# A planned attention and two-layer kernel: the first two batches regrouped by head halves and tile pairs, and the weight loads reordered

## The chip, the cores and the metric

The kernel runs on one core of a Trainium2 chip. The metric is the device time of one execution in microseconds (us). The engines named below are TensorE (PE: matmuls and transposes; PEld is its weight load), VectorE (DVE), ScalarE (ACT), GpSimd (POOL) and SyncE (SP), which only starts transfers. Transfers are started by SP (inputs of the attention, transposes by DMA) and by POOL (weights, which are cast from float32 to float16 on the way, and stores).

## The reference

```python
def phi(x, c, s):
    r = np.maximum(x, 0.0)
    return np.concatenate([r * c, r * s], axis=-1)
q_p = phi(q, cos_w, sin_w)
k_p = phi(k, cos_w, sin_w)
kv = np.einsum('bhsf,bhsd->bhfd', k_p, v)
z = np.sum(k_p, axis=2)
num = np.einsum('bhsf,bhfd->bhsd', q_p, kv)
den = np.einsum('bhsf,bhf->bhs', q_p, z)[..., None] + 1e-06
x = num / den          # 8 batches, 8 heads, 576 tokens, 64 per head
h = x @ w_in           # 4608 tokens x 512, 512 x 2048
g = h * np.cos(h)
out = g @ w_out        # 2048 x 512
```

The attention is linear: per head, one 128 x 65 product of k and v (the 65th column sums k), and a numerator with its denominator for every tile of tokens. Its result, transposed, is the input of a two-layer network.

## The kernel before

The kernel is written as a list of steps. Each step is added to a `Plan` with its engine, the functions that issue its instructions, and the keys that it reads and writes. Two tables in the source, `STARTS` (one whole number per step) and `ENGS` (one letter per step, for steps that either of two or three engines can do), give the order: steps are issued in the order of `STARTS`, on the engine of `ENGS`. Every engine runs its own instructions in that order and waits, in order, for what each needs.

Tokens: a batch has 576 tokens, four full tiles of 128 and a fifth of 64. Raw q, k and v lie in `km`, `qm` and `vm` (float32, one buffer each, used by all batches in turn), so a batch's k can be loaded only when the batch before has prepared its own. Each raw tensor of a batch is loaded by two transfers per group of heads, `go4` (line 339) and `go5` (line 336).

A batch's attention:
- `prep` (lines 368 on ACT, 369 on DVE) makes relu(x) times cos or sin, float16, into `KQ`; one instruction per tile and per cos or sin, over 8 heads or over a half of them.
- `cast_v` (382 ACT, 383 DVE, 384 POOL) casts v to float16.
- `kv` multiplies k and v over five tiles for 8 heads: 40 matmuls (line 397), and copies the result to `kvz`.
- `q_pe` transposes q of one tile on PE, 8 transposes (428), and copies it to `qT` (435 ACT, 437 DVE). Batches 2 and later do it by DMA (`q_dma`, 441).
- `num` makes the numerators of one tile (464), 8 matmuls in two banks; a normalisation on DVE follows, three instructions: the denominator (481), its reciprocal (483) and the product (485) into `XN`.
- `x_pe` transposes the result, 4 transposes (519), and a copy puts it into `xT` (522 to 524).

The network: `layer1` for batches 0 and 1 runs 16 groups of 8 matmuls (575), each group with a cosine on ACT (547) and a product on DVE (549). `layer2_plain` is the second layer of batch 0: for each of four tiles 16 matmuls (878) in two runs, over the first `WQ` quarters of `w_out` and over the rest; the first run is copied by ACT (886), the second added by DVE (889). Batches 1 to 8 use a form with seven products (`layer1_fast`, `layer2`), whose sums of weights are made on DVE: `w_out_sums` (901) and `w_in_sums` (660).

Before the weights come, PE runs dummy matmuls (`warm`, line 1041): 28 at the start, 17 after the first q transposes, and small groups between the numerators.

Loads of weights: `w_in` and `w_out` come in four quarters each, started by POOL. Small copies on POOL (1055, 1058, 1076, 1083) write one element of the destination first, so that a load waits for what the copy reads. `hold_raw` (1098) holds batch 1's inputs in the same way until `GATE1`, a quarter of a weight, has landed; `part_of_w_out` (1115) holds the last quarters of `w_out` until q or k of batch 1 has landed. Before, the order is: q, k, v of batch 0; four quarters of `w_in`; two of `w_out`; k, q, v of batch 1 (held until the quarter 2 of `w_in` is there); the other two of `w_out`.

The option `HH` chooses between `first_attention` (empty, as before) and `first_attention_halves`.

Of the kernel before, what the change touches and what calls it, by code (L numbers as in the profile page):

```python
# [13 lines left out]
F16 = mybir.dt.float16  # L14
# [3 lines left out]
OPT = dict(F16=0, WS2=[3, 1], HQ=[1, 0, 1], AQ=0, W2F=0, WQ=2, L2F=0, WFI=None, XPE=[0, 1, 2, 3, 4], FAST1={3:  # L18
           2, 4: 2, 5: 2, 6: 4, 7: 4, 8: 4}, MODE={}, HH='', LD=[['k', 0], ['v', 0], ['q', 0], ['k', 1], ['v',
           1], ['q', 1]], NB=[['A0', 'A1'], ['A0', 'A1', 'M0']], XB=[['B3'], ['B3', 'M1']], W0=5, W1=6,  # L20
           WF=[[2, 2, 2, 2], [2, 2, 0, 0]], HOLD=['k', 1], P0=0, RAW1=2, WO2=1, H1=0, DA=0, W2=0, SQ=0, NUZ=1)
# [169 lines left out]
def kernel(  # L191
# [84 lines left out]
    TR = ppool.tile([P, SM], F32, name="TR")  # L276
# [339 lines left out]
    FAST1 = OPT["FAST1"]  # L616
# [845 lines left out]
```

## Time and profile before

| | us |
|---|---|
| median of 3 runs | 281.5 (281.26 to 281.94) |
| the profiled execution | 281.42 |
| its span | 279.6 |
| PE busy | 272.5 |
| DVE busy | 236.4 |
| ACT busy | 210.0 |
| POOL busy | 83.4 |

The granted clock of PE is 1.00 over the whole span. The page gives busy times as shares of the span; in its rows of 40 slices a digit is the busy share of a slice of about 7 us in tenths. In rows of the timeline the first number is the start in us from the start of the span, the second the time taken, then the engine, the source line, the operation, what it writes and reads, how many instructions are merged, and in brackets the idle time before it and what ended it. An engine name with a q (SPq, POOLq) is the starting of a transfer. In rows of the DMA view the last number is the time in us from the starting of a transfer to its landing. In rows of windows, each engine has its busy time and its number of instructions, and the last three numbers are the granted clock, the busy share of the DMA engines and GB/s.

### The profile page before, as it was taken

The page shows a single profiled execution, that of the slowest core. Times are in us where ns is not written, and L with a number is a line of the kernel's source. Part 1 is how long each engine was busy: PE and PEld are TensorE (multiplying, and loading weights), DVE is VectorE, ACT ScalarE, POOL GpSimd, SP SyncE. Part 2 cuts the span into 40 slices and gives each one's busy share as a digit, 9 for nine tenths or more (in the row PEclk, how much of TensorE's full clock was granted, in tenths as well). Part 3 has the DMA queues.
Part 4 walks back from the last instruction along what each step waited for, and adds up shares of the span by engine and source line. Part 5 has one row for each costly group of instructions (what it writes and reads, how often), then busy time and mean ns, then how long its engine had stood idle before and what let it go on. Part 6 is the DMA issues. An engine that isn't in the chain of part 4 may idle for free.

```text
span 279.6 us, 6829 instructions
## 1 busy us (share of the span) xinstructions
PE 272.5 (97%) x2698; PEld 215.5 (77%) x2698; DVE 236.4 (85%) x442; ACT 210.0 (75%) x363; POOL 83.4 (30%) x104
## 2 busy tenths in 40 slices
PE   8999999999999999999999999999999999999993
PEld 2567867787966677769776878789988888888882
DVE  1767698989999999999999998989989879873952
ACT  2756699879998897788989978995758696776330
POOL 1340020030502101520440045132534372399210
PEclk9999999999999999999999999999999999999999
DMA  6999999989999999969999998739756495697125
GB/s 209 337 205 205 361 218 258 338 282 181 324 303 263 242 230 264 285 200 287 216 249 265 212 260 283 109 104 142 161 76 146 102 159 102 150 146 123 75 77 150
DMA packets 80223, 58.03 MB, mean 208 GB/s; under 512 B 43200, under 2 KB 77248, under 8 KB 80192
## 3 DMA queue, kind: packets, MB, share of 16 engines
q1 hardware_dynamic: 68960, 39.99, 59.3%
q0 software_dynamic: 10496, 17.04, 29.3%
q10 hardware_dynamic: 736, 0.57, 0.7%
q8 instruction: 21, 0.34, 0.5%
q14 instruction: 10, 0.08, 0.1%
HBM read 36.75 MB, written 11.80 MB: 174 GB/s over the span
## 4 chain that ended last, share of the span: by engine, by line
PE 92%; ACT 3%; DVE 2%; issue 1%; POOL 0%; ACTq 0%; POOLq 0%
PE M L953 34%; PE M L736 14%; PE M L608 11%; PE M L575 9%; PE TR L736 6%; PE ATT L1041 5%; PE ATT L464 3%; PE M L878 3%; PE ATT L397 3%; PE TR L608 2%; ACT KQ L368 1%; DVE XN L485 1%; PE M L428 1%; ACT V L382 0%; ACT ch L547 0%
## 5 line engine op out<-in xcount | busy, mean ns | idle before, releaser
L953 PEld LDWEIGHTS <-gT 128*128 128x128 f16 x560 | 53.9, 98 | 8.3
L953 PE MATMUL M<-w_out_sb,gT 128*128 128x256 f16 x448 | 57.1, 273 | 0.0
L549 DVE TENSOR_TENSOR gT<-M,ch 128x512 f16<-128x512 f32 x73 | 48.5, 684 | 5.9 <-ACT ch L547 5.7
L547 ACT ACTIVATE ch<-M 128x512 f32<-128x512 f32 x75 | 43.4, 596 | 12.2 <-PE M L575 5.4
L368 ACT ACTIVATE KQ<-km,CS 128x512 f16<-128x512 f32 x57 | 38.5, 718 | 1.6 <-DMA km<-in_k_dram 1.6
L964 ACT ACTIVATE ost<-M 128x512 f32<-128x512 f32 x41 | 24.3, 596 | 18.0 <-PE M L953 13.0
L368 ACT ACTIVATE KQ<-qm,CS 128x512 f16<-128x512 f32 x46 | 31.5, 721 | 4.0 <-DMA qm<-in_q_dram 4.0
L608 PE MATMUL M<-xT,w_in_sb 128*128 128x512 f16 x136 | 33.8, 379 | 0.0
L953 PE MATMUL M<-T,S 128*128 128x256 f16 x256 | 32.3, 273 | 0.0
L384 POOL CAST V<-vm 128x1024 f16<-128x1024 f32 (+1 forms) x18 | 15.8, 904 | 51.6 <-DVE den L481 21.6
L736 PEld LDWEIGHTS <-w_in_sb 128*128 128x128 f16 x288 | 27.3, 98 | 4.8 <-issue 0.3
L575 PE MATMUL M<-xT,w_in_sb 128*128 128x256 f16 x256 | 30.3, 273 | 0.3 <-DVE gT L549 0.3
L953 PEld LDWEIGHTS <-S 128*128 128x128 f16 x256 | 24.8, 98 | 4.1 <-DVE S L929 0.2
L575 PEld LDWEIGHTS <-w_in_sb 128*128 128x128 f16 x256 | 24.4, 98 | 3.9 <-issue 0.5
L748 DVE TENSOR_TENSOR Z<-M,Z 128x512 f32<-128x512 f32 x31 | 21.1, 687 | 4.3 <-PE M L736 3.2
L608 PEld LDWEIGHTS <-w_in_sb 128*128 128x128 f16 x160 | 14.9, 98 | 12.2
L549 POOL TENSOR_TENSOR gT<-Z,ch 128x512 f16<-128x512 f32 x5 | 6.3, 1268 | 56.6 <-ACT ch L547 20.0
L485 DVE TENSOR_TENSOR XN<-ATT,rec 128x512 f16<-128x512 f32 x32 | 22.1, 692 | 1.1
L464 PEld LDWEIGHTS <-qT 128*128 128x128 f16 (+1 forms) x320 | 14.8, 101 | 5.6 <-issue 3.5
L759 ACT ACTIVATE ch<-Z 128x1024 f32<-128x1024 f32 x12 | 12.7, 1057 | 6.9 <-DVE Z L748 4.9
L744 ACT ACTIVATE Z<-M 128x512 f32<-128x512 f32 x26 | 15.2, 596 | 3.4 <-PE M L736 2.4
L464 PE MATMUL ATT<-kvz,qT 128*128 128x65 f16 (+1 forms) x288 | 16.0, 195 | 0.8 <-DVE XN L485 0.5
(152 smaller groups left out, 519.3 us busy)
## 6 DMA issues: line engine op xcount, KB each, us to landing
out_dram<-ost POOLq DMA_DIRECT2D x38, 256.0 KB, 4.1
qm<-in_q_dram SPq DMA_DIRECT2D x8, 640.0 KB, 6.3
km<-in_k_dram SPq DMA_DIRECT2D x8, 640.0 KB, 7.1
qm<-in_q_dram SPq DMA_DIRECT2D x8, 512.0 KB, 5.7
km<-in_k_dram SPq DMA_DIRECT2D x8, 512.0 KB, 5.9
vm<-in_v_dram SPq DMA_DIRECT2D x6, 640.0 KB, 6.0
vm<-in_v_dram SPq DMA_DIRECT2D x6, 512.0 KB, 4.4
w_in_sb<-in_moe_w_in_dram POOLq DMA_DIRECT2D x4, 512.0 KB, 7.5
```

Source lines behind the costliest of these rows:

```text
L368: fn = {"ACT": lambda: nc.scalar.activation(out=out_, in_=in_, func=AF.Relu, scale=sc), "DVE": lambda: nc.vector.tensor_scalar(out=out_, i ...
L384: "POOL": lambda: nc.gpsimd.tensor_copy(out=out_, in_=in_)}
L464: nc.tensor.matmul(bank[hb][ps, hh * D1:(hh + 1) * D1], lhsT=x[:, h, :], rhs=z[:, h, :], start=True, stop=True)
L485: nc.vector.tensor_tensor(out=split(x16[n][:, hs, :], k), in0=A[:, :, :, 0:D], in1=split(rec[n][:, hs], k).unsqueeze(3).broadcast_to((P, k ...
L547: act(0.5, due, lambda: nc.scalar.activation(out=ch[c], in_=bank, func=AF.Sin, bias=math.pi / 2.0, scale=1.0), [key], [("ch", c)])
L549: mul(due, 0.61, lambda q: q.tensor_tensor(out=dst, in0=bank if len(dst.shape) == 2 else bank.rearrange("p (j s) -> p j s", j=dst.shape[1] ...
L575: nc.tensor.matmul(M1[m][:, jj * 2 * P:(jj + 1) * 2 * P], lhsT=w_in_sb[:, cc, j * P:(j + 1) * P], rhs=X[:, cc, ts], start=(cc == 0), stop= ...
L608: nc.tensor.matmul(M, lhsT=w_in_sb[:, cc, j * P:(j + 1) * P], rhs=X[:, cc, :], start=(cc == 0), stop=(cc == NCT - 1))
L736: nc.tensor.matmul(bank[0][:, j * TH:(j + 1) * TH], lhsT=a(cc, j), rhs=b[:, cc, :], start=(first and j == 0 and cc == 0), stop=(last and j ...
L748: dve(0.61, due + 0.3, lambda: nc.vector.tensor_tensor(out=dst, in0=bank[0], in1=dst, op=ALU.add), [bank[1], key], [key])
L953: nc.tensor.matmul(bank[0][:, tt * MH:(tt + 1) * MH], lhsT=a[:, j, tt * P:(tt + 1) * P], rhs=b[:, j, :], start=(first and (apart or tt == ...
L964: act(0.5, due, lambda: nc.scalar.activation(out=dst, in_=view(bank), func=AF.Copy), [bank[1]], dk)
```

## The change

The options and the two tables are new, and the order of the steps with them. The new options are `HH='kv'`, `P0=1`, `H1=2`, `WQ=3`, `W2F=2`, `RAW1=4`, `HOLD=['k', 0]`, another order `LD` of batch 0's loads and other numbers of dummy matmuls (`WF`). In words:

- Batch 0 runs `first_attention_halves`. q is prepared and transposed for all heads as before. k and v are prepared for heads 0 to 3 first; their product (`kv_half`, 20 matmuls) follows, then the numerators of a pair of tiles for these heads (`num_pair`), one normalisation for the pair, and four transposes and one copy for the pair (`x_pair`); then the same for heads 4 to 7. In the plan's order the two halves are interleaved. Both halves of the bank `ATT` hold a pair.
- Batch 1 uses `kv_half` and `num_pair` as well, and its steps may go to ACT or DVE.
- The first layer of batches 0 and 1 takes the groups of quarters 0 and 1 for the first half of the tokens, then for the second half, then quarters 2 and 3.
- Three quarters of `w_out` are loaded ahead of batch 1's inputs, which are held until the first quarter of `w_out` is there. The last quarter is held until the first transfer of batch 1's q has landed, through two copies on POOL.
- Batch 0's second layer is split into runs of 12 and 4 matmuls.
- The dummy matmuls are five groups of four and small groups of two.
- The code gains an option `FW`, which is not used.

Loads of batch 0 stay in the order q, k, v with v in two halves of heads.

```diff
-OPT = dict(F16=0, WS2=[3, 1], HQ=[1, 0, 1], AQ=0, W2F=0, WQ=2, L2F=0, WFI=None, XPE=[0, 1, 2, 3, 4], FAST1={3:
-           2, 4: 2, 5: 2, 6: 4, 7: 4, 8: 4}, MODE={}, HH='', LD=[['k', 0], ['v', 0], ['q', 0], ['k', 1], ['v',
-           1], ['q', 1]], NB=[['A0', 'A1'], ['A0', 'A1', 'M0']], XB=[['B3'], ['B3', 'M1']], W0=5, W1=6,
-           WF=[[2, 2, 2, 2], [2, 2, 0, 0]], HOLD=['k', 1], P0=0, RAW1=2, WO2=1, H1=0, DA=0, W2=0, SQ=0, NUZ=1)
+OPT = dict(F16=0, WS2=[3, 1], HQ=[1, 0, 1], AQ=0, FW=None, W2F=2, WQ=3, L2F=0, WFI=None, XPE=[0, 1, 2, 3, 4],
+           FAST1={3: 2, 4: 2, 5: 2, 6: 4, 7: 4, 8: 4}, MODE={}, HH='kv', LD=[['q', 3], ['k', 3], ['v', 0],
+           ['v', 1]], NB=[['A0', 'A1'], ['A0', 'A1', 'M0']], XB=[['B3'], ['B3', 'M1']], W0=5, W1=6, WF=[[2,
+           2], [2, 2]], HOLD=['k', 0], P0=1, RAW1=4, WO2=1, H1=2, DA=0, W2=0, SQ=0, NUZ=1)
 STARTS = (
...
 ENGS = (
...
-        warm(28, 9.05)
+        if OPT["FW"]:
+            for i, n in enumerate(OPT["FW"]):
+                warm(n, 7.5 if i == 0 else 0.2157 * n)
+        else:
+            warm(28, 9.05)
...
-        warm(17, 3.67, rd=[("TR", 0)])
+        if not OPT["FW"]:
+            warm(17, 3.67, rd=[("TR", 0)])
```

The functions that the new options call, which were in the file before:

```python
def kv_half(hb, bank, key, due, b=0):
    hs = range(H)[HALVES[hb]]
    def mm():
        for hh, h in enumerate(hs):
            for t in range(NT + 1):
                nc.tensor.matmul(
                    bank[:, hh * D1:(hh + 1) * D1], lhsT=kp[:, t, h].rearrange("p g d -> p (g d)"),
                    rhs=V1[:, t, h, :], start=(t == 0), stop=(t == NT))
...
    copy_by_either(Z[:, hb], bank[:, 0:HB * D1], due, 0.4, 0.38, [key], [("kvz", b, hb)])

def num_pair(i, hb, due, b=0):
    for t in (2 * i, 2 * i + 1):
        bank, key = ATT[:, t % 2, :], ("ATT", t % 2)
...
    A = ATT[:, :, 0:HB * D1].rearrange("p t (h d) -> p t h d", h=HB)
    def norm():
        nc.vector.tensor_scalar_add(out=denp[:, n], in0=A[:, :, :, D], scalar1=1e-6)
        nc.vector.reciprocal(out=recp[:, n], in_=denp[:, n])
        nc.vector.tensor_tensor(out=XF[:, hb, 2 * i:2 * i + 2], in0=A[:, :, :, 0:D],
                                in1=recp[:, n].unsqueeze(3).broadcast_to((P, 2, HB, D)), op=ALU.mult)
    dve(1.05, due, norm, [("ATT", 0), ("ATT", 1)], [("XF", b, i, hb)] + ([("XF", 0, i, hb)] if b else []))

def half_tiles(hb, due):
    for nm in OPT["HH"]:
        if nm == "k":
            for t in range(NT + 1):
                for g in range(2):
                    prep(0, "k", t, g, "", due, hs)
        elif nm == "v":
            for t, nt in ((0, 2), (2, 2), (4, 1)):
                cast_v(0, t, ("DVE", "ACT", "POOL"), due, hs, nt=nt)
            kv_half(hb, *BANKS2[hb], due)
...
    if hb == 0:
        for i in range(OPT["W1"]):
            warm(2, 0.4314, ATT[:, 1, :], [("TR", 0)] if i == 0 else [], [("ATT", 1)])
    if OPT["P0"]:
        for i in range(NT // 2):
            num_pair(i, hb, due + 2 * i)
            n = OPT["WF"][hb][i]
            if n:
                warm(n, 0.2157 * n, M1[1], [("ATT", 1)], [("M1", 1)])
            x_pair(i, hb, *pick[kb_[i % len(kb_)]], due + 2 * i)
        return
```

More of the change, by code (lines that the diff above doesn't have):

```diff
@@ L24 @@
 STARTS = (
[98 rows of a table removed]
[99 rows of a table added]
 )
 ENGS = (
-    "DDPSSSSSSSSDAPDDDPADAPDDAPAGGGGPDADADDDADADADADDADADGGGGGGPPADPPDPPAPPDPPAPPDPPAPPDPAPAD"
-    "PADPADPADPADPADPADPADPADPADPADPADPADPADPADPADGSSGSSGGGGGSSSSDADADADADADAPDDAPADAPDDAPADA"
-    "DADADDADADPPAPPDPAPPDPAPPDPAPPDPAPDPPDPAPAPAPAPAPDPDGGPDPDGGPADPADPADPADPADPADPADPADPADP"
-    "ADPADPADPADPADPADPADDDDDSSSSSSADADAADDAAGGGPPADASDDSAASAASPPDPAPPDPAPPDPAPPDPADDDPPAPPDD"
-    "PPAPPAPPDPPDGGPPAGGPADPADPADPADPADPADPADPADPADPADPADPADPADPADPADPADSSSSSSDDAAAAAAAAGGGPP"
@@ L130 @@
-    "ADASAASDASAASADPPDSPPDSPPDSPPDSSPPDSDDDDDDDPPAPPDDPPAPPAPPDPPDGGPPAGGDDDDPAPDAGPAPAPDPDA"
-    "DPADPADPADPADPADPAPDAGPAPAPDPDADPADPADPADPADPADSSSSSSAAAAAADAAAGGGPPAAASAASAASADSPPDSPPD"
-    "SPPDSPPDSDDDPPAPPDDPPAPPAPPDPPDGGPPAGGDDDDPAPDAGPAPAPDPDADPADPADPADPADPADPAPDADPAPAPDPDA"
-    "DPADPADPADPADPADSSSSSSDDAAAAAAADGGGPPAADSAASDDSAASAAPPDSPPDSPPDSPPDSSPPDSDDDPPAPPADPPAGG"
-    "PPAPPAPPAGGPPAGGGGDDDDPAPDAGPAPAPDPDADPADPADPADPADPADPAPDADPAPAPDPDAGPADPADPADPADPADSSSS"
-    "SSAAAAAAADAAGGGPPAAASADSADSAASPPDSPPDSPPDSPPDSDDDDDDDPPAPPADPPAGGPPAPPAPPAGGPPAGGGGDDDDP"
@@ L136 @@
-    "APDADPAPAPDPDADPADPAPDAGPAPAPDPDAGPADPAPDADPAPAPDPDADPADPAPDADPAPAPDPDADPADSSSSSSDAAAAAA"
-    "AAAGGGPPADASDASAASDDSAAPPDSPPDSPPDSPPDSSPPDSDDSPPAPPAGGPPAGGPPAPPAPPAGGPPAGGGGDDDDPAPDAG"
-    "PAPAPDPDAGPADPAPDADPAPAPDPDADPADPAPDADPAPAPDPDADPADPAPDADPAPAPDPDADPADDDDDSPPAPPDGGPPAPP"
-    "APPDPPDGGPPAGGDDDDPAPDAGPAPAPDPDAGPADPAPDAGPAPAPDPDAGPADPAPDAGPAPAPDPDADPADPAPDAGPAPAPDP"
-    "DADPADDDDDDDPPAPPDDDPPAPPAPPDPPDSASAAPPDSADSA"
+    "DDPPPPPSSSSSSSSDDPADDPAADPDDAPAGGGGAADDDADDADDDAPAPPPPPPPPDPPAPPDPPAADADDAADDDADAPAPPDPP"
@@ new lines @@
+    "APPDPPDGGGGGGGPADPADPADPADPADPADPADPADPADPADPADPADPADPADPADPADGSSGSSGGGGGSSSSDADDDDADADD"
+    "APDDAPAADPDDDPADDDADADDPDPAPPDPAPPDPAPPDPAPPDPAPAPPDPAPAPAPAPAPDPDGGPDPDGGPADPADPADPADPA"
+    "DPADPADPADPADPADPADPADPADPADPADPADDDDDSSSSSSADAAAAADDAGGGPPAADSADSAASAASPPDPAPPDPAPPDPAP"
+    "PDPADDDPPAPPDDPPAPPAPPDPPDGGPPAGGPADPADPADPADPADPADPADPADPADPADPADPADPADPADPADPADSSSSSSA"
+    "DAAAAAAADGGGPPADASDASAASAASAAPPDSPPDSPPDSPPDSSPPDSDDDDDDDPPAPPDDPPAPPAPPDPPDGGPPAGGDDDDP"
+    "APDAGPAPAPDPDADPADPADPADPADPADPAPDAGPAPAPDPDADPADPADPADPADPADSSSSSSAAAAAAAAADGGGPPAAASAA"
@@ new lines @@
+    "SAASADSPPDSPPDSPPDSPPDSDDDPPAPPDDPPAPPAPPDPPDGGPPAGGDDDDPAPDAGPAPAPDPDADPADPADPADPADPADP"
+    "APDADPAPAPDPDADPADPADPADPADPADSSSSSSAAADAAAADDGGGPPAAASAASDASAASDAPPDSPPDSPPDSPPDSSPPDSD"
+    "DDPPAPPADPPAGGPPAPPAPPAGGPPAGGGGDDDDPAPDAGPAPAPDPDADPADPADPADPADPADPAPDADPAPAPDPDAGPADPA"
+    "DPADPADPADSSSSSSAAAAAAADAAGGGPPAAASADSADSAASPPDSPPDSPPDSPPDSDDDDDDDPPAPPADPPAGGPPAPPAPPA"
+    "GGPPAGGGGDDDDPAPDADPAPAPDPDADPADPAPDAGPAPAPDPDAGPADPAPDADPAPAPDPDADPADPAPDADPAPAPDPDADPA"
+    "DSSSSSSDAAAAAAAAAGGGPPADASDASAASDDSAAPPDSPPDSPPDSPPDSSPPDSDDSPPAPPAGGPPAGGPPAPPAPPAGGPPA"
@@ L141 @@
+    "GGGGDDDDPAPDAGPAPAPDPDAGPADPAPDADPAPAPDPDADPADPAPDADPAPAPDPDADPADPAPDADPAPAPDPDADPADDDDD"
+    "SPPAPPDGGPPAPPAPPDPPDGGPPAGGDDDDPAPDAGPAPAPDPDAGPADPAPDAGPAPAPDPDAGPADPAPDAGPAPAPDPDADPA"
+    "DPAPDAGPAPAPDPDADPADDDDDDDPPAPPDDDPPAPPAPPDPPDSASAAPPDSADSA"
 )
```

197 rows, old and new, of the table STARTS are left out of this document.

## The prediction

> **What bounds the kernel now.** I read the page's shares first, then the chain of waits, then the timeline and the DMA view of the stretch that the change rebuilds (the first 56 us).
>
> ```profile
> PE 272.5 (97%) x2698; PEld 215.5 (77%) x2698; DVE 236.4 (85%) x442; ACT 210.0 (75%) x363; POOL 83.4 (30%) x104
> PE   8999999999999999999999999999999999999993
> DMA  6999999989999999969999998739756495697125
> PE 92%; ACT 3%; DVE 2%; issue 1%; POOL 0%; ACTq 0%; POOLq 0%
> ```
>
> TensorE (PE) is busy in every slice and is 92% of the chain that ended last. The end is therefore the sum of three things: when PE starts the first layer of batch 0, how much PE work stands behind that start, and how long PE waits in it. Each edit is priced by what it does to one of the three; the profiled execution (281.42 us, of which 279.6 are the span) is the base. The front of before, where the first term is set:
>
> ```profile
> 10.73 2.20 DVE L369 TENSOR_SCALAR KQ<-km,CS 128x512 f16<-128x512 f32 x5 [1.51 <-DMA km<-in_k_dram]
> 12.85 0.69 DVE L383 CAST V<-vm 128x256 f16<-128x256 f32 x3
> 16.52 0.43 DVE L412 CAST kvz<-M 128x260 f16<-128x260 f32 x1 [1.25 <-PE M L397]
> 19.16 0.69 DVE L485 TENSOR_TENSOR XN<-ATT,rec 128x512 f16<-128x512 f32 x1
> 19.91 0.29 PE L464 MATMUL ATT<-kvz,qT 128*128 128x65 f16 x4 [0.50 <-DVE XN L485]
> 20.03 0.39 PE L519 MATMUL TR<-IDENT,XN 128*128 128x128 f16 x4
> 20.45 0.60 ACT L524 ACTIVATE xT<-TR 128x512 f16<-128x512 f16 x1 [0.41 <-PE TR L519]
> 20.51 0.29 PE L464 MATMUL ATT<-kvz,qT 128*128 128x65 f16 x4
> 20.84 0.17 DVE L481 TENSOR_SCALAR den<-ATT 128x8 f32<-128x8 f32 x1 [0.98 <-PE ATT L464]
> 21.10 1.03 PE L575 MATMUL M<-xT,w_in_sb 128*128 128x256 f16 x8
> 21.27 0.69 DVE L485 TENSOR_TENSOR XN<-ATT,rec 128x512 f16<-128x512 f32 x1
> 22.02 0.40 PE L519 MATMUL TR<-IDENT,XN 128*128 128x128 f16 x4
> 23.13 0.39 PE L519 MATMUL M<-IDENT,XN 128*128 128x128 f16 x4
> ```
>
> Read as handovers: a normalisation (L481 to L485) runs from 20.84 to 21.96, 1.12 us; PE goes on 0.06 later (19.85 to 19.91); numerator matmuls that start at 20.51 let DVE start at 20.84, 0.33 later. Transposes to copy is 0.42 (20.03 to 20.45), copy to the first layer 0.65 (20.45 to 21.10). The first layer starts at 21.10.
>
> Second and third term, up to the matmuls of batch 0's second layer at 52.38:
>
> ```profile
> 23.78 10.72 PE M L575 x96
> 48.18 1.73 PE M L878 x8
> 49.90 0.45 PE M L519 x8
> 52.10 0.45 PE M L428 x8
> 60.20 0.60 PE ATT L397 x20
> 23.78 10.71 PE L575 MATMUL M<-xT,w_in_sb 128*128 128x256 f16 x96 [0.26 <-DVE gT L549]
> 44.23 0.29 PE L464 MATMUL ATT<-kvz,qT 128*128 128x65 f16 x4 [0.24 <-ACT kvz L415]
> 52.38 1.89 PE L878 MATMUL M<-w_out_sb,gT 128*128 128x512 f16 x8
> ```
>
> The first five rows, from the chain, are prices of PE work when nothing is waited for: a first-layer group of eight (10.72 less the 0.16 us in which the last one drains, over 12 groups) 0.88, a second-layer matmul 0.216, eight transposes 0.45, half a k-v product 0.60; four numerators are 0.13. Between 21.10 and 52.38 PE does 18 groups (15.84), 40 second-layer matmuls (8.65), five q transposes (2.25), two halves of k-v (1.20), eight fours of numerators (1.04) and six fours of x transposes (1.35), 30.33 together, in 31.28 us. So PE waited about 0.95, part of it in the two idle marks above.
>
> **Part 1: batch 0 by head halves and tile pairs; the fillers.** The two blocks of 28 and 17 dummy matmuls become small groups; they stand in PE's waits before the first layer and cost nothing unless one delays the matmul behind it. Two of them sit between rounds, 0.43 us each, and end before the round's normalisation does (1.12). The loads keep their order (q, k, v in two halves), so k is there at 10.73 as before. DVE then has seven half-head k preparations and two two-tile casts ahead of the first half product. No half-head preparation stands in the trace. Bounds: the half-head cast, 0.69 us for three (0.20 each), and the full preparation, 2.20 for five (0.41 each). I take 0.24, near the cast, which has the same shape: 10.73 + 7 x 0.24 + 2 x 0.4 = 13.2, and the half product starts at 13.35.
>
> From there: product 0.60, drain and handover 0.20, copy to kvz 0.43 (row at 16.52) and 0.05, so 14.6 for the first pair of numerators. Each round then is 0.13 + 0.33 + 1.12 + 0.06 = 1.64, because both halves of ATT hold one pair and the next pair must wait for the normalisation. In before two rounds overlap, as other banks take part. The first layer needs the left half of xT for all heads, so the third round: 14.57 + 3 x 1.64 = 19.49, plus 0.42 and 0.65: it starts at 20.56. Gain 0.54. Bounds: with 0.20 preparations and fours that overlap the round (1.51) 20.0; with full-price preparations 21.7.
>
> Behind the start, before still runs two fours of x transposes for batch 0 (22.02, 23.13), after only one: 0.22 less work.
>
> The first layer of a batch now goes through its 16 groups half of the tokens first; the groups are the same.
>
> **Part 2: three quarters of w_out ahead of batch 1.** The rows:
>
> ```profile
> q0 software_dynamic: 445, 0.45, 123.6%
> 24.00:28.00 4.00, 4.00 (x39) 3.44 (x37) 2.73 (x4) 2.67 (x5) 0.54 (x4) 1.00 1.24 205
> 28.00:36.00 8.00, 8.00 (x68) 6.45 (x66) 5.87 (x10) 5.79 (x11) 0.00 (x0) 1.00 1.08 361
> 24.98 0.60 SPq L339 DMA_DIRECT2D km<-in_k_dram  x1
> 25.70 0.60 SPq L336 DMA_DIRECT2D km<-in_k_dram  x1
> km<-in_k_dram SPq DMA_DIRECT2D x1, 640.0 KB, 7.7
> 26.34 0.63 SPq L339 DMA_DIRECT2D qm<-in_q_dram  x1
> qm<-in_q_dram SPq DMA_DIRECT2D x1, 512.0 KB, 8.5
> 32.17 0.62 SPq L336 DMA_DIRECT2D vm<-in_v_dram  x1
> vm<-in_v_dram SPq DMA_DIRECT2D x1, 320.0 KB, 7.6
> 36.80 0.18 POOL L1115 CAST w_out_sb<-qm 2x2 f16<-2x2 f32 x1 [11.49 <-DMA qm<-in_q_dram]
> 37.28 1.90 POOL L1093 DMA_DIRECT2D w_out_sb<-in_moe_w_out_dram  x2 [0.30 <-POOL w_out_sb L1115]
> ```
>
> The first row is the DMA view of 25.6 to 27.8 us: batch 1's k was issued at 24.98 and 25.70, yet the weights' queue q0 is the only one that moves. The queues drain in the order of issue, and by the page's DMA row they are full from the second slice (7 us each) to beyond batch 1's loads. So a quarter (524 KB at 205 GB/s: 2.56 us) put ahead moves all of batch 1's inputs by 2.56, wherever their gate opens: k from 25.70 + 7.7 = 33.4 to 35.95, first half of q from 34.85 to 37.4, v from 39.8 to 42.35. The gate itself moves from a quarter of w_in to the first of w_out and opens later, still inside the backlog; on SP only batch 2's loads stand behind it.
>
> What covers it: the 12-to-4 split. Four groups of 12 second-layer matmuls (2.60 each) now stand ahead of batch 1's first transposes. PE's stream from 20.56: 16 groups 14.08, a four of transposes 0.22, 4 x 2.60, two q transposes 0.90 and the product 1.20, to 47.36; q transposes are first due at 45.3. DVE and ACT (seven preparations each on DVE from 36.0 at 0.41, q's behind them, v casts until 43.8) end before that, so the shift is hidden with 1.5 us to spare. The split itself moves 32 of 64 matmuls and adds none; the evacuations keep their number.
>
> The last quarter now waits on the first half of q through one more hop: issued at 37.4 + 0.15 + 0.25 + 0.5 = 38.3, it drains behind v and lands at 42.35 + 2.56 = 44.9. On POOL only stores and batch 2's casts stand behind that wait, due after 50. DVE stands behind it in order: the w_out sums (1.22, below), then a q copy (0.69), both due before the kvz copy at 47.56, so it may land up to 45.65. Margin 0.7.
>
> **Part 3: batch 1 by pairs.**
>
> ```profile
> 44.03 0.69 DVE L437 COPY qT<-M 128x1024 f16<-128x1024 f16 x1
> 49.94 0.69 DVE L889 TENSOR_TENSOR ost<-M,ost 128x512 f32<-128x512 f32 x1
> 50.55 1.22 DVE L901 TENSOR_TENSOR T<-w_out_sb 128x2048 f16<-128x2048 f16 x1
> ```
>
> k-v issue ends at 47.36, kvz is copied by 47.99, numerators start at 48.05; the q transposes between end at 47.81, so PE waits 0.24. DVE then runs, in order: a k preparation of batch 2, four normalisations, a q copy, two second-layer adds. The add at 49.94 is followed 0.61 later, so back to back an instruction costs 0.07 less than its row. Batch 2's k is issued when the last k preparation frees its buffer (39.1) and drains behind the quarter: 44.9 + 1.18 MB at 361 GB/s = 48.2. Preparation 0.41, then 1.05 + 0.66 + 1.05 + 0.61 + 1.05 + 0.61 + 1.12, to 54.8. PE has, between 48.05 and the transposes behind that: 1.00 numerators, 0.90 q, 0.67 x, 3.46 in four more groups, 6.03, to 54.1: it waits 0.8. ACT, held by the same k until 48.2, may cost a copy 0 to 0.4; I take 0.2. Sum 1.2 against 0.95. From there PE does the same work and waits for little; I carry the offset to the end.
>
> **The rule that speaks against it.** The Trainium skill, DMA: Bandwidth & Descriptors, section on queues, rings and completion order, says that each DMA engine takes turns between the queue rows that have work, packet by packet. The row of 25.6 to 27.8, one queue alone with another waiting, disagrees here.
>
> **Sum.** 281.42 - 0.54 - 0.22 + 0.25 = 280.9; the median shown, 281.5, is 0.1 from the base, which I leave out.
>
> **Rivals.**
> A, all of the front arrives: start at the low bound 20.0 (-1.1), 0.22 less, DVE's chain hidden so that only the 0.24 is waited for (-0.7): 279.4. For it: PE saturated behind 24 us; against: 1.64 per round is in rows. 0.17.
> B, half heads buy nothing: preparations at full price, start 21.7: +0.6 - 0.22 + 0.25, 282.05. Against: the cast's 0.20. 0.14.
> C, slower: the last quarter and batch 2's k (issued at 38.3 and 39.1, 0.8 apart) share the engines. Alone the quarter takes 2.56, shared about 5.1: it lands at 47.5, decisive once past 45.65. DVE's in-order queue holds sums, q copy and kvz copy until 49.85, 1.9 late: 282.8. For it: the margin is a sum of eight estimates; against: q0 alone in the row above. 0.17. (By the skill's turn-taking this is what happens.)
> D, the offset is eaten later, by transfers of q of batch 2 or stores that now come earlier: within 0.3% of before. 0.05.
>
> **Chances.** Forecast 0.47, own range 280.2 to 281.7. A measurement of this kernel tells 0.3% (0.84 us) from no change. Faster: half of the forecast's and all of A, 0.41; slower: C and what B and the forecast leave above, 0.21; same 0.38. The range, to A and C: 279.2 to 282.9.
>
> **What would show it.** First layer at 20.4 to 20.7 in the timeline; 1.64 between DVE's first normalisations; k preparations of batch 1 at 36.0; DVE's first w_out sum at about 45.0 and no DMA gap near 38 to 40; PE's first numerators of batch 1 at 48.05. Wrong if the sum starts after 45.7, if the first layer starts before 20.2, or if waits appear behind 56 us.

## The result and the profile after

| | before | changed |
|---|---|---|
| median, us | 281.5 (281.01 to 281.94, 9 runs) | 283.07 (281.92 to 284.08, 9 runs) |
| the profiled execution | 281.42 | 283.07 |
| its span | 279.6 | 280.9 |

The ratio is 1.0061, with a 95% interval of 1.0045 to 1.0076: slower, where 280.9 was forecast. Two later sets of runs of the unedited changed kernel gave medians of 282.43, ratio 1.0036 (1.0019 to 1.0054), and 282.63, 1.0038 (1.0022 to 1.0054). So the loss is 1.0 to 1.6 us. A few slower runs (one of `rerun`, one of `kbehind`, two of `mended`, two of before) are left out of the medians and ratios.

The page after, its shares first, then the slices of PE, then the chain of waits by engine:

```profile
PE 270.3 (96%) x2684; PEld 213.8 (76%) x2684; DVE 235.9 (84%) x435; ACT 211.6 (75%) x365; POOL 83.3 (30%) x105
PE   8889999998999999999999999999999999999993
PE 85%; DMA 6%; DVE 5%; ACT 1%; SPq 1%; issue 1%; DVEq 0%
```

PE does less (270.3 against 272.5 us) and ends later. The chain goes through DMA for 6%, where before's names none. The tenth slice of PE, about 63 to 70 us, lost a tenth. The timeline shows where the loss ends; the first row is of before, the second of the changed kernel, the same step:

```profile
192.15 1.91 PE L953 MATMUL M<-w_out_sb,gT 128*128 128x256 f16 x16
```

```profile
193.38 1.91 PE L954 MATMUL M<-w_out_sb,gT 128*128 128x256 f16 x16
```

From about 139 us to the end, where both kernels' steps have the same order, every step of PE is later by the same 1.23 to 1.24. All that the change does to the span is done by then. Less the starts of the first layer (21.10 and 20.86) the two rows are 171.05 and 172.52 us behind it: the start was 0.24 earlier, and what follows took 1.47 longer.

The waits of PE in windows (start and end, length, then PE's busy time and count; the other engines, clock, DMA share and GB/s follow). Before:

```profile
40.00:58.00 18.00, 17.75 (x211) 12.32 (x209) 16.90 (x44) 15.76 (x29) 2.42 (x3) 1.00 0.99 262
58.00:80.00 22.00, 22.00 (x278) 18.63 (x276) 20.18 (x38) 20.39 (x37) 4.92 (x8) 1.00 1.07 300
```

Changed:

```profile
40.00:58.00 18.00, 17.22 (x202) 11.48 (x202) 14.52 (x35) 14.77 (x25) 0.54 (x1) 1.00 0.90 267
58.00:80.00 22.00, 20.93 (x274) 18.14 (x267) 20.00 (x40) 20.57 (x39) 6.75 (x9) 1.00 1.09 278
```

PE idles 0.78 in the stretch of batch 1's attention (0.25 before), and 1.07 in the next (none before). In the two later profiles of the changed kernel (`rerun`, `rerun2`, below) it idles 1.00 and 1.30 in the first stretch and almost nothing in the second. The waits view names the causes, with us, times and the longest:

```profile
PE ATT L465 <- DMA qT<-KQ: 1.1, 1, 1.1
PE ATT L1184 <- ACT kvz L1163: 0.5, 1, 0.5
```

The 1.1 is one wait for a transpose by DMA of batch 2. The 0.5 at L1184 is the second half of batch 1's k-v product.

### The profile page after: what moved, and what is told of

It is laid out like the page before. It is cut to its first block, busy times and chain, and to the rows that moved or that the text cites. A ratio compares the mean times of both kernels' runs of the same rounds, so it can differ in the third digit from the quotient of the medians.

```text
span 280.9 us, 6820 instructions
## 1 busy us (share of the span) xinstructions
PE 270.3 (96%) x2684; PEld 213.8 (76%) x2684; DVE 235.9 (84%) x435; ACT 211.6 (75%) x365; POOL 83.3 (30%) x105
## 4 chain that ended last, share of the span: by engine, by line
PE 85%; DMA 6%; DVE 5%; ACT 1%; SPq 1%; issue 1%; DVEq 0%
PE M L954 34%; PE M L737 14%; PE M L609 11%; PE M L576 7%; PE TR L737 6%; PE M L879 4%; DMA qT<-KQ 3%; DMA km<-in_k_dram 3%; PE ATT L465 3%; PE ATT L398 2%; PE TR L609 2%; DVE KQ L370 2%; DVE XN L1245 1%; PE ATT L1236 1%; DVE gT L550 1%
## 5 line engine op out<-in xcount | busy, mean ns | idle before, releaser
L369 ACT ACTIVATE KQ<-km,CS 128x512 f16<-128x512 f32 (+1 forms) x60 | 39.6, 692 | 2.7 <-DMA km<-in_k_dram 2.7
L749 DVE TENSOR_TENSOR Z<-M,Z 128x512 f32<-128x512 f32 x31 | 21.1, 687 | 5.0 <-PE M L737 3.8
L486 DVE TENSOR_TENSOR XN<-ATT,rec 128x512 f16<-128x512 f32 x28 | 19.4, 691 | 1.0
L822 POOL DMA_DIRECT2D out_dram<-ost x20 | 11.1, 554 | 23.7 <-DVE ost L890 16.9
L835 POOL DMA_DIRECT2D out_dram<-ost x12 | 13.3, 1202 | 11.1 <-ACT ost L965 11.1
```

The source lines that it names most:

```text
L369: fn = {"ACT": lambda: nc.scalar.activation(out=out_, in_=in_, func=AF.Relu, scale=sc), "DVE": lambda: nc.vector.tensor_scalar(out=out_, i ...
L486: nc.vector.tensor_tensor(out=split(x16[n][:, hs, :], k), in0=A[:, :, :, 0:D], in1=split(rec[n][:, hs], k).unsqueeze(3).broadcast_to((P, k ...
L749: dve(0.61, due + 0.3, lambda: nc.vector.tensor_tensor(out=dst, in0=bank[0], in1=dst, op=ALU.add), [bank[1], key], [key])
```

## The experiments

There are fifteen more profiles, four of them of unedited kernels. A number of the table in an edit is a step's place in the order of issue: a larger number, a later place.

**The unedited kernels again.** `rerun` and `rerun2` are the changed kernel, `before_again` and `before_third` the one before; no line is edited.

> The changed kernel again, unedited. Theory 'room': the new order gives the transposes of q of batch 2, which go through the DMA queues, 7 us from issue to the numerators that read them, and in this stage all DMA queues now and then stand still for 1 to 2 us; PE's wait ahead of the second numerators of batch 2 (1.07 us in the first profile) is there when a standstill falls on the second transposes and otherwise is below 0.2 us. Time 282 to 284. Rival 'stores': the wait is there each time, since the stores of batch 0 share the queues with the transposes each time.

> The changed kernel, unedited, beside room2 on one chip. Theory 'room': 282.6 to 283.1, waits for a transpose in batch 2 or 3 of 0 to 1.1; first normalisation of batch 1 0.52 to 0.54 behind the landing of batch 2's k. Rival: same median as room2.

> The kernel before, unedited, one more profile. Theory 'room': its numerators of batches 2 and 3 come 1.7 to 3.9 us behind the landing of the transposes that they read; standstills of all DMA queues of 1 to 2 us occur here too, and PE waits less than 0.2 for any transpose. Rival: waits of 0.5 or more for a transpose of q stand here too, and the room is not the difference.

> The kernel before, a third profile. Theory 'filler': the first layer starts between 20.7 and 21.1, 9.9 to 10.4 behind the start of k's preparations, as its k-v product begins on its casts (14.7) or on the end of the filler block (15.1). PE's waits for transposes 0 to 0.4.

Measured: the two ratios above; before 281.59 and 280.55 in one run each. Start of the first layer, and from it to the step of the two rows above:

| profile | start | behind it |
|---|---|---|
| before | 21.10 | 171.05 |
| before_again | 20.71 | 171.56 |
| before_third | 20.21 | 171.03 |
| changed | 20.86 | 172.52 |
| rerun | 20.73 | 171.93 |
| rerun2 | 20.99 | 172.06 |

The base of the forecast, 21.10, is the latest start of three; their mean is 20.67, the changed kernel's 20.86. Eight of the nine edited kernels with the new order (below) start between 20.63 and 21.09, 20.87 in the mean; the ninth, `kbehind_split`, starts at 23.26 (last section). Why before varies is seen in the timeline of before_again and then of before_third:

```profile
10.60 3.83 PE L1041 MATMUL ATT<-S 128*128 128x512 f16 x17
20.71 1.03 PE L575 MATMUL M<-xT,w_in_sb 128*128 128x256 f16 x8
```

```profile
10.10 3.83 PE L1041 MATMUL ATT<-S 128*128 128x512 f16 x17
20.21 1.03 PE L575 MATMUL M<-xT,w_in_sb 128*128 128x256 f16 x8
```

The block of 17 dummy matmuls begins when the first q transposes are done, lasts 3.83, and the first layer follows 10.11 behind its begin in both, as in the first profile (10.99 and 21.10). The forecast let k's preparation set the front of before; the block did.

**The front alone.** `front_alone` is the kernel before with the changed front; its later steps keep their relative order. The edit is shown against the changed kernel, without the tables and the lines that give batch 1 back its old engines and casts:

```diff
-OPT = dict(F16=0, WS2=[3, 1], HQ=[1, 0, 1], AQ=0, FW=None, W2F=2, WQ=3, L2F=0, WFI=None, XPE=[0, 1, 2, 3, 4],
+OPT = dict(F16=0, WS2=[3, 1], HQ=[1, 0, 1], AQ=0, FW=None, W2F=0, WQ=2, L2F=0, WFI=None, XPE=[0, 1, 2, 3, 4],
...
-           2], [2, 2]], HOLD=['k', 0], P0=1, RAW1=4, WO2=1, H1=2, DA=0, W2=0, SQ=0, NUZ=1)
+           2], [2, 2]], HOLD=['k', 0], P0=1, RAW1=2, WO2=1, H1=0, DA=0, W2=0, SQ=0, NUZ=1)
...
```

> Part 1 alone: batch 0 as in the changed kernel (head halves, tile pairs, small fillers) ahead of the rest as in the kernel before (two quarters of w_out ahead of batch 1, second layer of batch 0 in 8 and 8, batch 1 by whole heads, gate on w_in). Theory 'sum': the first layer starts at 20.75 to 20.9 instead of 21.10, a four of x transposes less stands behind it, nothing else moves: 0.45 to 0.6 less than before, 280.9. Rival 'inputs': the inputs of batch 1 land no earlier, so that PE waits at batch 1's transposes and product (39 to 44 us) for what it gained: 281.4.

Measured: 281.74, ratio 1.0016 (1.0001 to 1.0030). Its timeline:

```profile
11.18 2.45 DVE L370 TENSOR_SCALAR KQ<-km,CS 128x256 f16<-128x256 f32 x7 [0.30 <-DMA km<-in_k_dram]
21.53 1.69 PE L576 MATMUL M<-xT,w_in_sb 128*128 128x256 f16 x14
192.35 1.91 PE L954 MATMUL M<-w_out_sb,gT 128*128 128x256 f16 x16
```

Behind the start it takes 170.82, 0.23 less than before (171.05): the term "0.22 less work" holds. The start does not gain: seven half-head preparations take 2.45 us, 0.35 each, and k landed late in this execution. Part 1 alone gains nothing. Behind the start the changed kernel takes 172.17 in the mean of its three profiles, 1.35 more than this one: the loss behind the start is in the rest of the change, parts 2 and 3.

**Batch 1: the order of product and copy.** `kvfirst` issues the second half of the product ahead of the copy of the first.

```diff
-    4200, 4176, 4567, 4629, 4504, 4566, 4681, 4694, 4706, 4863, 4969, 4838, 4850, 4880, 5022, 5080,
+    4200, 4176, 4565, 4629, 4504, 4566, 4681, 4694, 4706, 4863, 4969, 4838, 4850, 4880, 5022, 5080,
```

> The second half of the k-v product of batch 1 is emitted ahead of the copy of the first half's result, not behind it; no data or engine changes. Theory 'tile': the 0.48 us wait of the second half is for that copy, since both halves are in the two banks of one PSUM tile: the halves then run back to back (wait below 0.1), the product ends at about 47.8 instead of 48.32, the copy of its result starts behind DVE's q copy (48.13), the first numerators start 0.3 earlier (48.6): time 0.2 to 0.3 less. Rival 'sums': the wait is for DVE's w_out sum, which ends at the same moment (47.53): the 0.48 stays and the time does not move.

Measured: 283.19, ratio 1.0061 (1.0036 to 1.0086). First the timeline of the changed kernel, then that of kvfirst:

```profile
46.30 1.23 DVE L902 TENSOR_TENSOR T<-w_out_sb 128x2048 f16<-128x2048 f16 x1 [2.66 <-DMA w_out_sb<-in_moe_w_out_dram]
46.31 0.77 PE L1184 MATMUL ATT<-V,KQ 128*128 128x65 f16 x20
47.56 0.76 PE L1184 MATMUL ATT<-V,KQ 128*128 128x65 f16 x20 [0.48 <-ACT kvz L1163]
48.16 0.61 PE L429 MATMUL M<-IDENT,KQ 128*128 128x128 f16 x8
48.92 0.41 PE L1236 MATMUL ATT<-kvz,qT 128*128 128x65 f16 x8
48.95 0.49 DVE L370 TENSOR_SCALAR KQ<-km,CS 128x512 f16<-128x512 f32 x1
49.37 0.17 DVE L1243 TENSOR_SCALAR den<-ATT 128x8 f32<-128x8 f32 x1
51.03 1.03 PE L879 MATMUL M<-w_out_sb,gT 128*128 128x512 f16 x4
52.19 0.41 PE L1236 MATMUL ATT<-kvz,qT 128*128 128x65 f16 x8
```

```profile
46.24 1.37 PE L1184 MATMUL ATT<-V,KQ 128*128 128x65 f16 x40
47.31 1.22 DVE L902 TENSOR_TENSOR T<-w_out_sb 128x2048 f16<-128x2048 f16 x1 [3.10 <-DMA w_out_sb<-in_moe_w_out_dram]
47.65 0.39 ACT L1163 ACTIVATE kvz<-ATT 128x260 f16<-128x260 f32 x1 [0.59 <-PE ATT L1184]
49.53 0.41 PE L1236 MATMUL ATT<-kvz,qT 128*128 128x65 f16 x8 [1.47 <-DVE kvz L1162]
```

The two halves lie in two banks of one tile, `ATT`. In the changed kernel the second half waits for the copy of the first (start to start 1.25 for 0.60 of work). With the order turned the product runs through, but the copy of the first half waits for the second (0.59 <-PE ATT), and the numerators start later, at 49.53; in this execution the quarter of `w_out` landed 1 us later too. Nothing is gained: the wait moved to the other side of the tile. The rival of the expectation, a wait for DVE's sum, is out: the product now ends at 47.61 and the sum runs to 48.53. That the common tile is the reason is read from the two waits; no run puts the halves into two tiles. kvfirst's edit stays in all later kernels of this part.

**The last quarter of w_out, and batch 2's k.** `klater` moves the last k preparation of batch 1 and with it the loads of batch 2's k.

```diff
-    3652, 3558, 3613, 3535, 3574, 3496, 3720, 3730, 3496, 3691, 3869, 3826, 4459, 4520, 3986, 3945,
+    3652, 3558, 3613, 3535, 3574, 3496, 3720, 4070, 3496, 3691, 3869, 3826, 4459, 4520, 3986, 3945,
-    7077, 7154, 7212, 7346, 7495, 4406, 5472, 7380, 8767, 3858, 3797, 4083, 4143, 4401, 4280, 4846,
+    7077, 7154, 7212, 7346, 7495, 4406, 5472, 7380, 8767, 4079, 4078, 4083, 4143, 4401, 4280, 4846,
```

> Against the changed kernel: the product's second half emitted ahead of the copy of the first (as before in kvfirst), and one preparation of batch 1's k moved behind those of q on DVE, so that batch 2's k is issued at about 43 instead of 39.3, when the last quarter of w_out is already moving. Theory 'shared': on the late sixteenths the quarter shares the DMA engines with that k; left alone it lands at 45.3 instead of 46.2 to 46.4, DVE's w_out sum starts at 45.4 and the first numerators at 48.2 instead of 48.8 to 49.0: 0.5 less than the changed kernel. Rival 'late sixteenths': the last of the sixteen parts of every transfer lag by 1.2 us since 31 us anyway, the quarter lands at 46.2 as before and the numerators stay at 48.7.

Measured: 283.6, ratio 1.0070 (1.0043 to 1.0097). DMA rows of the quarter's issue (KB, us to landing), the changed kernel and then klater, and klater's timeline of DVE:

```profile
w_out_sb<-in_moe_w_out_dram POOLq DMA_DIRECT2D x1, 512.0 KB, 7.4
```

```profile
w_out_sb<-in_moe_w_out_dram POOLq DMA_DIRECT2D x1, 512.0 KB, 6.2
```

```profile
45.04 1.23 DVE L902 TENSOR_TENSOR T<-w_out_sb 128x2048 f16<-128x2048 f16 x1 [1.20 <-DMA w_out_sb<-in_moe_w_out_dram]
50.20 0.16 DVE L1243 TENSOR_SCALAR den<-ATT 128x8 f32<-128x8 f32 x1
```

The quarter was issued at 38.7 in both. With k issued 3.5 us later (42.83 and 43.48 for 39.26 and 39.91) it lands at 44.9, as forecast, for 46.2. In all ten profiles in which k is issued 0.5 us behind the quarter, the quarter takes 7.3 to 8.0 us to land, for 6.2 here. So it shares the engines with k: rival C's mechanism, in half of its size (1.3 late for 2.6). Only its end is shared: of its 528 packets 480 have moved by 44.0 us in the changed kernel and 518 in `klater`; the last 48 move by 47 us, among 957 on the queue of the attention's loads. The Trainium skill (DMA: Bandwidth & Descriptors, section on queues, rings and completion order) has each engine take turns between the queues with work, and the last tenth of the quarter agrees with it. How much an engine takes in one turn, no run here shows. But k lands 0.84 later, DVE's first normalisation follows it as before, and the kernel is no faster.

**Half of the sum, half of the hold.** `sumsplit` makes the third sum of `w_out_sums` in two halves, of which only the second, at place 5465, needs the last quarter.

```diff
-        tt(T3, b22, b12, ALU.subtract, wk, ["T3"])
+        h = JH // 2
+        tt(T3[:, 0:h], b22[:, 0:h], b12[:, 0:h], ALU.subtract, [wk[0], wk[2]], [("T3", 0)])
+        tt(T3[:, h:], b22[:, h:], b12[:, h:], ALU.subtract, [wk[1], wk[3]], ["T3"])
```

> Against the changed kernel: the product's second half emitted ahead of the copy of the first, and the first w_out sum in two halves: the half that needs no last quarter runs in DVE's idle time at 43.7, the other behind the numerators, ahead of the second sum. Theory 'quarter': DVE's q copy no longer stands behind the landing of the last quarter; it starts at 46.6, the kvz copy at 47.7, the first numerators of batch 1 at 48.2 instead of 48.8 to 49.0; of that 0.3 to 0.6 stays at 59 us, time 0.3 to 0.6 less than the changed kernel. Rival 'DVE full': DVE has no gap between 46 and 63, so the half sum is paid back there and PE at 59 us stands where it did (within 0.15).

Measured: 283.2, ratio 1.0064 (1.0039 to 1.0088). DVE no longer waits for the quarter; its first normalisation stands at 50.23, 0.52 behind the landing of batch 2's k at 49.71. In all seven profiles of these orders up to here that distance is 0.52 to 0.54: a k preparation stands ahead of the normalisation. Two readings were left: k's landing holds DVE, or DVE is full anyway.

**The preparation behind the normalisations.** `kbehind` is kvfirst with the k preparation of batch 2 on DVE moved behind them, one on ACT too.

```diff
-    5316, 5303, 5018, 4907, 5241, 4628, 4663, 5394, 4784, 5774, 5664, 5604, 5938, 6000, 6062, 5130,
+    5316, 5303, 5018, 4907, 5241, 4700, 5314, 5394, 4784, 5774, 5664, 5604, 5938, 6000, 6062, 5130,
```

`kbehind_split` adds sumsplit's edit, `mended` that and numlater's (below).

> Against the changed kernel: the product's second half emitted ahead of the copy of the first (kvfirst), and the two preparations of batch 2's k that stand ahead of batch 1's first normalisation are moved: DVE's behind the last of the four normalisations, ACT's behind the next q copy. Theory 'k landing': in all seven profiles so far DVE's first normalisation of batch 1 began 0.52 to 0.54 behind the landing of batch 2's k (48.8 to 50.0), through that one preparation ahead of it on DVE; without it the normalisation begins 0.35 behind the first numerators, at 48.9 to 49.1, wherever k lands, and the first layer of batch 1 at 53.9 to 54.1 instead of 54.3 to 54.6: 0.3 to 0.4 less than the changed kernel. Rival 'DVE full': DVE is short of work nowhere between 46.3 and 63, the preparation is paid back behind, and PE's numerators for the fifth tile (57.8 to 58.1) do not move by more than 0.15.

> kbehind and sumsplit together: neither k's landing nor that of the last quarter stands ahead of batch 1's numerators on DVE, and half of the sum runs in DVE's idle time ahead of 46. If these two landings are what the batch's rounds wait for, the first numerators start at 48.1 to 48.3, the normalisation at 48.5 to 48.7 and the first layer of batch 1 at 53.4 to 53.7: 0.7 to 0.9 us ahead of the changed kernel, of which at least 0.5 stays at 59 us. Rival 'DVE full': the numerators start early but PE at 59 us gains below 0.3.

> kbehind_split with the second numerators of batch 2 two first-layer groups later (numlater). If the transposes' room is what is left, time lies at or below that of kbehind_split, 281.4 to 282.0, with no wait above 0.3 for a transpose of batch 2; batch 3's transposes keep their room of 0.5 to 1 us and may still be waited for (0 to 1 us). Rival: what batch 1 gains is lost whole at the transposes of batches 2 and 3, whose issue does not move, and the time stays at 282.5 or above.

Measured: kbehind 282.78, ratio 1.0058 (1.0034 to 1.0082); kbehind_split 283.44, 1.0064 (1.0040 to 1.0089); mended 282.94, 1.0061 (1.0041 to 1.0081). The timeline of kbehind:

```profile
49.05 0.17 DVE L1243 TENSOR_SCALAR den<-ATT 128x8 f32<-128x8 f32 x1 [0.50 <-PE ATT L1236]
54.00 1.04 PE L576 MATMUL M<-xT,w_in_sb 128*128 128x256 f16 x8
59.09 2.12 PE L576 MATMUL M<-xT,w_in_sb 128*128 128x256 f16 x18 [0.21 <-DVE gT L550]
192.53 1.91 PE L954 MATMUL M<-w_out_sb,gT 128*128 128x256 f16 x16
```

The normalisation no longer follows k: k landed at 49.33, and it began at 49.05, released by the numerators. Batch 1's first layer starts at 54.00 (54.32 in the changed kernel, at nearly the same start), and this profile is the best of the family, 192.53 at the late step. So k's landing did hold DVE, by 0.3 us here. More profiles say the same: from the start of the first layer of batch 0 to that of batch 1 it is 33.16 us in all four kernels with the moved preparation (these three and `room2`, below), and 33.46 to 34.06 in the five that have the changed kernel's order here (it, `rerun`, `rerun2`, `numlater` and `storelate`). But little of it stays. The preparation now stands behind the normalisations, and PE waits for DVE ahead of the step at 59.09, which starts at 59.05 in the changed kernel; counted from the start, kbehind and room2 are at 38.25 and 38.26 there, the five at 38.19 to 38.83, and with the split sum as well (kbehind_split, mended) at 38.98 and 38.99. So both readings hold: k's landing held DVE, and what is moved out of its way DVE pays back at the next place. The medians do not tell these kernels apart.

**Batch 2 and 3: the transposes by DMA.** The new table issues batch 2's transposes 1.4 us earlier, but places its second numerators at 67.0 for 69.3. Timeline of the changed kernel, then of before:

```profile
58.31 5.79 SPq L442 DMA_TRANSPOSE qT<-KQ  x3
63.98 0.42 PE L465 MATMUL ATT<-kvz,qT 128*128 128x65 f16 x8
68.08 0.30 PE L465 MATMUL ATT<-kvz,qT 128*128 128x65 f16 x4 [1.07 <-DMA qT<-KQ]
```

```profile
59.73 6.03 SPq L441 DMA_TRANSPOSE qT<-KQ  x3
67.34 0.42 PE L464 MATMUL ATT<-kvz,qT 128*128 128x65 f16 x8
69.34 0.42 PE L464 MATMUL ATT<-kvz,qT 128*128 128x65 f16 x8
```

From issue to first use the first transpose had 7.6 us (59.73 to 67.34) and has 5.7. The second took 8.2 us to land (issue row below). The DMA view of 58 to 70 us, in 40 slices of 0.3 us, shows why:

```profile
qT<-KQ SPq DMA_TRANSPOSE x1, 8.2
GB/s 92 113 294 375 389 354 352 377 384 393 381 352 276 134 182 284 288 240 291 465 437 192 266 203 15 0 0 2 9 15 221 225 140 383 94 211 384 349 406 378
```

From slice 25, about 65.2 us, almost nothing moves for 1.8 us. The same view of before has such a standstill too, at 64 us; there no matmul was waiting. `numlater` puts batch 2's second numerators behind two groups of the first layer; `storelate` moves the last three stores of batch 0, which could be what stops the engines, behind them.

```diff
-    6558, 6458, 6648, 6855, 6878, 6878, 6977, 6990, 7164, 7297, 7199, 7187, 7215, 7386, 7444, 6534,
+    6672, 6660, 6690, 6855, 6878, 6878, 6977, 6990, 7164, 7297, 7199, 7187, 7215, 7386, 7444, 6534,
```

```diff
-    6289, 3636, 3895, 3290, 3620, 4155, 4413, 3895, 4154, 4885, 5149, 4752, 4984, 5223, 5872, 5590,
-    5990, 5058, 5930, 6064, 6119, 5211, 5507, 5586, 5453, 5554, 5646, 5366, 5603, 5705, 5676, 5775,
+    6289, 3636, 3895, 3290, 3620, 4155, 4413, 3895, 4154, 4885, 5149, 4752, 4984, 5223, 7065, 5590,
+    5990, 5058, 5930, 7066, 7067, 5211, 5507, 5586, 5453, 5554, 5646, 5366, 5603, 5705, 5676, 5775,
```

`room2` is kbehind and numlater, and the same move for batch 3:

```diff
-    8273, 8325, 8226, 8339, 8574, 8523, 8510, 8535, 8939, 8796, 8895, 9002, 9240, 9167, 9266, 9288,
+    8273, 8325, 8226, 8339, 8574, 8613, 8612, 8645, 8939, 8796, 8895, 9002, 9240, 9167, 9266, 9288,
```

> The second numerators of batch 2 stand two first-layer groups and a four of transposes later on PE (1.97 us of work). Theory 'room': the 1.07 us wait ahead of them is gone (below 0.2) and nothing else moves, since the rounds are 3.1 us apart and the chain of one is 1.7: 1.0 us less, 282.0. Rival 'eaten later': the wait turns up again at the next numerators or at the first layer of batch 2, time 283.0.

> The last three stores of batch 0 are issued behind a cast of V of batch 3, at 75 instead of 61 to 64 us. Rival 'stores': without their packets the second transposes land about 6 us after their issue, by 66, and the wait of 1.07 is gone: 282.0. Theory 'room': the queues still stand still for 1 to 2 us at about 64 us (as in the kernel before, which has no store there) and the wait stays where that falls on the second transposes: 282.5 to 283.1, wait 0.5 to 1.1.

> kbehind with the second numerators of batch 2 two first-layer groups later (numlater) and the second numerators of batch 3 one second-layer group (1 us) later, so that both stand further behind the transposes that they read. Theory 'room': kbehind's profile had no wait for a transpose and took 282.2, its median was 282.9, the difference being such waits in other executions; with the room the median falls to 282.0 to 282.4 and the profile shows no wait for a transpose above 0.2. Rival: the waits go on to the third numerators or the first layer of batch 3 and the median stays at 282.7 to 283.

Measured: numlater 282.86, ratio 1.0051 (1.0031 to 1.0071); storelate 282.82, 1.0065 (1.0039 to 1.0092); room2 282.68, 1.0054 (1.0034 to 1.0074), beside rerun2's 282.63 on the same chip. One timeline row each, of storelate and of room2:

```profile
88.51 0.43 PE L465 MATMUL ATT<-kvz,qT 128*128 128x65 f16 x8 [0.89 <-DMA qT<-KQ]
```

```profile
91.26 0.30 PE L465 MATMUL ATT<-kvz,qT 128*128 128x65 f16 x4 [0.57 <-DMA qT<-KQ]
```

Where rounds have room, their wait is gone (but `rerun`, without any edit, has none there either), and another round of batch 3 waits instead: the second pair in storelate (and, for 0.5, in numlater), the third in room2. Taking the stores away did not take the wait out of the kernel. Of twelve profiles with the new table's later part, seven show such a wait of 0.2 to 1.07; of five with the old one, one (0.4, in batch 4). In rerun and rerun2 it is under 0.1: the table runs closer to a landing time that varies, and pays sometimes.

**A smaller block of dummies.** Since the block of 17 sets before's start, `fill15` is the kernel before with two fewer.

```diff
-        warm(17, 3.67, rd=[("TR", 0)])
+        warm(15, 3.24, rd=[("TR", 0)])
```

> The kernel before with 15 dummy matmuls instead of 17 in its second filler block. Theory 'filler': in the first profile of before the block ended so late that the k-v product stood behind it (15.11), in the second it ended 0.4 earlier and the product began at 14.71 on its casts; with two dummies less (0.43) the product begins on its casts in every execution, the first layer 9.9 to 10.0 behind the landing of k's last part, and the time is 0.1 to 0.4 less than before: 281.0 to 281.3. Rival 'inputs': the casts of V set the product anyway, the start stays where it is and the time is the same.

Measured: 281.21 (280.45 to 282.07), ratio 0.9992 (0.9978 to 1.0006): not told apart from before. Its timeline:

```profile
9.97 3.40 PE L1041 MATMUL ATT<-S 128*128 128x512 f16 x15
19.97 1.03 PE L575 MATMUL M<-xT,w_in_sb 128*128 128x256 f16 x8
191.65 1.91 PE L953 MATMUL M<-w_out_sb,gT 128*128 128x256 f16 x16
```

The first layer starts at 19.97, the earliest of all, 0.70 ahead of before's mean, but what follows takes 171.68, 0.47 above before's mean of 171.21: in this execution two thirds of the earlier start are lost behind it. The block is 0.43 shorter, but from its begin to the first layer it is only 0.11 less (10.00 for 10.11): behind the block something else holds the rest, so a still shorter one has little to gain here.

## Why the prediction was wrong

**The bound** was read rightly: PE's start, its work and its waits account for the time, and the loss is in start and waits. The forecast was 0.5 less than before and the means of the profiles are 1.3 more. Of these 1.8 us the start makes 0.73 (part 1), the waits behind it 0.93 (part 3, in which part 2 has a share, and what came behind 56 us), and 0.15 lies outside the span.

**Part 1, the start: 20.56 forecast, 20.86 measured.** The timeline of the changed kernel:

```profile
10.58 2.38 DVE L370 TENSOR_SCALAR KQ<-km,CS 128x256 f16<-128x256 f32 x7
13.78 0.76 PE L1184 MATMUL M<-V,KQ 128*128 128x65 f16 x20 [0.57 <-DVE V L384]
15.02 0.41 PE L1236 MATMUL ATT<-kvz,qT 128*128 128x65 f16 x8
16.65 0.41 PE L1236 MATMUL ATT<-kvz,qT 128*128 128x65 f16 x8 [0.79 <-DVE XN L1245]
18.29 0.43 PE L1236 MATMUL ATT<-kvz,qT 128*128 128x65 f16 x8
20.86 1.91 PE L576 MATMUL M<-xT,w_in_sb 128*128 128x256 f16 x16
```

The step "I take 0.24, near the cast" failed: a half-head preparation takes 0.34, nearer the bound at 0.41, and the numerators start at 15.02 for 14.57 (the working's own terms add up to 14.63). The rounds of 1.64 were right (15.02, 16.65, 18.29). The base was too late as well: 21.10 was the latest of three starts, 20.67 their mean. So the gain of 0.54 was a loss of about 0.2, between the forecast and rival B (preparations at full price, a start at 21.7).

**"0.22 less work"** was right, by the front alone (0.23).

**Part 2.** The inputs' delay was hidden, as said: the transposes of batch 1 run on time. The last quarter, put at 44.9, landed at 46.2, beyond the limit of 45.65, and DVE's sum started at 46.30, one of the signs named as wrong. The step that failed is that the queues drain in the order of issue: k of batch 2, 0.5 us behind, took a share of the end. The row of 25.6 to 27.8 us, from which the order was inferred and by which the rule of turns was set aside, could not decide it: about one quarter was left on q0, the weights' queue, then (445 packets there and 113 behind 27.8), k's queue moved from 27.9, and the two ran side by side to 30. Rival C's 282.8 is near the measured time, but by luck: it lets the late quarter delay the batch by 1.9 us, and with DVE free of the quarter (`sumsplit`) the first numerators start at 48.66 for 48.92, not 0.3 earlier.

**Part 3: 1.2 forecast for the waits up to 56 us, 1.7 to 2.3 measured.** From rows, start to start less the prices of the prediction: the first product half 0.65 (46.31 to 47.56, for 0.60), the q transposes ahead of the first numerators 0.31 (48.16 to 48.92, for 0.45; forecast 0.24), the group of four at 51.03 0.30 (1.16 for 0.86), and small ones. rerun2 adds 0.5 before its second pair:

```profile
51.29 0.42 PE L1236 MATMUL ATT<-kvz,qT 128*128 128x65 f16 x8 [0.52 <-DVE XN L1245]
```

The 0.65 was missed altogether: the forecast let the halves of the product follow one another, though both lie in `ATT`. Before's own waits, 0.95 in the forecast, come to about 1.1 by the same sum: right.

**"From there PE does the same work and waits for little"** failed: the working followed the new table only to 56 us. Of the 1.44 by which the profiled execution is longer behind the start than forecast, 1.07 is the transpose wait at 68.08. Rival D, which let an offset be eaten later, pointed to this place but not to a loss.

**The account.** Means of three profiles each: start +0.19, behind the start +0.96, and outside the span +0.15 (time less span: medians 2.0 for the changed kernel, 1.85 for before, over all runs), 1.3 together, against medians 1.0 to 1.6 apart. The 0.96 is made of -0.23 work, about +0.94 in batch 1's attention and about +0.25 later. With three profiles these shares are good to some 0.3 us (an estimate, from how far the profiles of one kernel lie apart). Shown by an experiment are the 0.23, that parts 2 and 3 hold the loss behind the start (one profile of `front_alone`), the wait between the halves of the product whichever comes first, the quarter's sharing with k, and k's hold on DVE. Not shown is a version that gets the loss back: nine edited kernels, which each take or shift one or more of these waits, all stay at 1.005 to 1.007. What the profiles say of the reason is that a wait taken out of batch 1 comes back as a wait for DVE by about 60 us; no run frees DVE itself, so this is argued. What stays open is also what fixes the landing of the transposes in batch 3, and why 0.15 more lies outside the span.

## What to carry to other kernels

A start taken from one execution is one draw (20.2 to 21.1 here): look for what sets it, here a fixed block of fillers, before booking a gain on it. When a table of starts is made anew, compare the room between issue and use of every transfer all the way to where the orders agree, not only in the stretch that the change names. An operation split into two banks of one tile waited here whichever half came first, so price such a wait before counting on the split.

## What the runs showed that was not expected

- DMA moves almost nothing for 1 to 2 us several times in an execution, in every kernel (65.2 to 67.0 in the changed kernel), and what starts them was not found. A transpose by DMA that lands in 4.6 us in one execution (storelate) takes 8.2 in another.
- Half the width of a preparation costs much more than half: 0.34 us for 128x256, 0.41 for 128x512.
- A queue that moves alone while another has been started does not show that transfers drain in the order of issue. In both stretches here the older transfer's bulk moved first and its end was shared (28 to 30 us in the kernel before; the last quarter, 7.4 us with k behind it and 6.2 without).
- Fewer fillers may leave the front open to a late input (one profile, and no run tests it). In that of `kbehind_split` batch 0's q was late (its preparation on DVE began at 8.76 us, at 7.31 in the changed kernel), PE had nothing to do for 3.15 us, and its granted clock from 10 to 16 us was 0.76, 0.50 and 0.88 by stretches of 2 us; the first layer started at 23.26, 11.30 behind k's preparations for 10.28. In the changed kernel, where PE waited 0.83 us there, the clock is 1.00 in the same stretches, as in all other profiles. In the kernel before the first block of fillers runs to 10.26.
- The time outside the span differs by kernel and execution, 1.74 to 2.2 us.
